# Reading the up products' tokens in turn, one store for a chunk, later reloads and a new order

## The chip, the cores and the metric

The kernel runs on one core of one Trainium2 chip. The metric is device time in microseconds (us), the median of several executions. An execution taken by the hardware profiler gives the trace from which the rows below are read.

## The reference

Two stages follow one another. The first is a gated recurrence for 4 batches, 8 heads, 768 tokens and 48 dimensions a head; the second is a feed-forward layer over the 3072 tokens, 384 wide inside and out, 2048 wide in the middle.

```python
for t in range(S):                                    # q, k, v, alpha: (4, 8, 768, 48)
    state = alpha[:, :, t, :, None] * state + np.einsum('bhd,bhe->bhde', k[:, :, t], v[:, :, t])
    y[:, :, t] = np.einsum('bhd,bhde->bhe', q[:, :, t], state)
x = y.transpose(0, 2, 1, 3).reshape(B * S, H * D)     # (3072, 384)
h = x @ w_in                                          # (3072, 2048)
sp = np.where(h > 20.0, h, np.log1p(np.exp(np.minimum(h, 20.0))))
out = (h * np.tanh(sp)) @ w_out                       # (3072, 384)
```

The weights come as 64-bit floats; everything else is 32-bit.

## The kernel before

**Chunks.** The recurrence is cut into 24 chunks. A chunk is 64 tokens of two batches at once: 128 rows, the first batch's 64 tokens and behind them the second's. For each chunk VectorE runs two scans over alpha and scales q and k, TensorE forms the scores, the products with v, the part from the state and the change of the state (lines 610, 633, 674, 755), and the 384 results of every token are written to the tile `xs` as an upper part and a remainder (lines 688 to 708). Six small transfers then put part of the rows in place (`move`, line 714).

**Units.** The feed-forward layer is cut into 106 units. A unit is one slice of 128 of the 2048 middle columns for two or four chunks, so 256 or 512 tokens. `up` (line 821) makes nine matmuls into one PSUM bank, three slices of the 384 inputs by three combinations of upper part and remainder, each with 256 or 512 columns of `xs` as the moving operand. ScalarE and VectorE then work on the result one after another: `exp` (line 830), `square` (833), `log` (836), `inverse` (839), `gate` on VectorE (842), `upper` (848), `lower` on VectorE (851). `down` (line 879) makes three matmuls of 384 columns for each chunk of the unit, with 128 tokens of `g` as weights; it gathers over the 16 slices in a PSUM bank of the chunk. After the last slice `result` (line 913) copies the bank to the tile `osb` (or adds to a part kept in SBUF first) and `store` (line 919) sends it to HBM in two transfers of 64 rows, one for each batch, because the two batches' tokens lie far apart in the output. Both go out on SyncE's queue (SP); for the last chunk, number 23, the second goes out on ScalarE's queue (`LAST_BY_ACT`).

**Weights.** Each of the 16 slices is loaded once (line 422), its 64-bit words are turned into an upper part and a remainder by VectorE and ScalarE (lines 437 to 480), and later it is loaded a second time (`wc`, line 495) for two sums by which ScalarE proves that the values fit the fast path (lines 504 and 507). The first loads and the reloads share two buffers, `stage`.

**Fillers.** Until a given time, TensorE is handed small matmuls without a use (line 937) where it would have nothing to do.

**The order.** Nothing is decided on the chip. A planner in the kernel's source walks through all tasks with a price for each (`COST`: time on the engine, time until others may use the result), a model of SP's queue (`SLACK` is added to each transfer's due time), and a key for each task: the number of the unit before which it is due plus a shift (`SHIFT`) found beforehand. On each engine the task that can begin first is next, and of several the one with the lowest key. `CHECK_FROM` and `CHECK_STEP` give the keys of the reloads, `EARLY_BANKS` says which PSUM banks a chunk uses. The order that comes out is what every engine then runs, strictly in that order: an instruction that waits for a transfer holds up everything behind it on its engine.

At the end the results of all checks are joined into one number, which decides whether a general path must run; it is not taken here.

Of the kernel before, what the change touches and what calls it, by code (L numbers as in the profile page):

```python
# [27 lines left out]
B, H, S, D = 4, 8, 768, 48  # L28
# [3 lines left out]
HALF = C // 2  # L32
# [31 lines left out]
CHECK_FROM = 45.0  # L64
# [6 lines left out]
    0: "o2 att att h h".split(),  # L71
    1: "att h o3 h att".split(),
    2: "o3 att o3 o0 o1".split(),
    3: "att att o3 o2 att".split(),
    4: "o0 att h".split(),
    7: "att o1 att".split(),
    8: "o3 att att".split(),
    9: "o1 att att".split(),
    10: "att o0 att".split(),
    11: "o2 att o1".split(),  # L80
    12: "o3 o0 att".split(),
    13: "h o1 att".split(),
    14: "o1 o0 o2".split(),
    15: "h att att".split(),
    16: "att h att".split(),
    17: "o0 h att".split(),
    18: "o0 att o2".split(),
    19: "o2 o0 att".split(),
    20: "att o2 att".split(),
    21: "att o1 o0".split(),  # L90
    22: "att o3 att".split(),
# [7 lines left out]
    },  # L99
    "unit": {  # L100
# [16 lines left out]
    },  # L117
    "weight": {
        0: -1.5121, 1: -4.3451, 2: -0.52089, 4: 0.30693, 5: 1.0304, 6: 3.2906, 7: 0.74523,
        8: 2.2474, 9: 2.1922, 10: 2.7782, 11: -2.8998, 12: 0.71473, 13: -2.0961, 14: 0.29398,  # L120
        15: -0.066785,
    },
    "weight check": {
        0: -0.41042, 1: -0.099631, 2: -3.9864, 3: 1.3786, 4: 0.10748, 5: 2.7189, 6: -0.74965,
        7: 3.7486, 8: 0.17213, 9: 2.0992, 12: 3.4975, 14: -1.471, 15: -6.7254,
    },
}
X_PE = 4
LAST_BY_ACT = (23,)
TURN_AT = 0.15  # L130
W_PE = 3
W_DVE = 3
# [160 lines left out]
SLACK, SLACK_FROM = (1.1, 0.4), 12.0  # L293
# [14 lines left out]
for _n in range(1, 5):  # L308
    _c = 128 * _n
# [896 lines left out]
```

## Time and profile before

| what | value |
|---|---|
| median of 3 runs | 509.14 us (508.57 to 509.17) |
| the profiled execution | 506.55 us |
| its span, first to last instruction | 504.8 us |
| mean granted clock of TensorE | 0.996 of full speed |
| TensorE busy | 487.5 us, 97% of the span |
| ScalarE busy | 393.2 us, 78% |
| VectorE busy | 323.9 us, 64% |
| moved by DMA | 56.83 MB |

The span leaves out what lies ahead of the first and behind the last instruction; the profiled execution took 1.75 us more than its span. The median of the timed runs lies 2.59 us above the profiled execution. A busy TensorE in this table includes the fillers, and the weight loads (431.5 us) overlap the matmuls.

### The profile page before, as it was taken

Reading aid. Unit: us, or ns where it says so; the run is one execution under the profiler, and the core shown is the slowest. Engines: PE = TensorE matmul, PEld = TensorE weight load, DVE = VectorE, ACT = ScalarE, POOL = GpSimd, SP = SyncE. Lnnn points to the kernel's source line nnn. Section 1 sums busy time; section 2 is a strip of 40 time slices with the busy share of each in tenths; the row PEclk is TensorE's granted clock in tenths of the full one; section 3 lists DMA queues with packets and bytes.
Section 4 is the critical chain, followed back from the end, with each engine's and each line's share of the span. In section 5 each row is a group of like instructions: output and inputs, shape, how many; then the busy total and the mean of one; then the engine's idle time right before and its main releaser. Section 6 shows DMA issues by size and latency. Waiting matters only on the chain.

```text
span 504.8 us, 12766 instructions
## 1 busy us (share of the span) xinstructions
PE 487.5 (97%) x5225; PEld 431.5 (85%) x5225; DVE 323.9 (64%) x632; ACT 393.2 (78%) x902; POOL 2.4 (0%) x12
## 2 busy tenths in 40 slices
PE   7979999999999998999999999999999999999993
PEld 4668999899998887889898889989888899889993
DVE  8989999999975777878534859323383333333231
ACT  2667988989989996979996677787666876886682
POOL 1000000000000000000000000000000000000000
PEclk9999999999999999999999999999999999999998
DMA  8765535433332755667410551000320000200002
GB/s 302 264 220 196 200 118 188 139 126 125 127 125 80 240 183 206 200 238 246 167 64 1 156 185 72 0 1 1 80 88 19 8 1 0 51 13 1 1 1 66
DMA packets 20463, 56.83 MB, mean 113 GB/s; under 512 B 4400, under 2 KB 12848, under 8 KB 20400
## 3 DMA queue, kind: packets, MB, share of 16 engines
q1 hardware_dynamic: 20320, 55.87, 33.0%
q8 instruction: 42, 0.69, 0.5%
q14 instruction: 21, 0.17, 0.1%
q10 hardware_dynamic: 80, 0.10, 0.1%
HBM read 48.87 MB, written 4.72 MB: 106 GB/s over the span
## 4 chain that ended last, share of the span: by engine, by line
PE 83%; DVE 5%; DMA 5%; ACT 2%; SPq 2%; issue 2%; DVEq 0%
PE bank L879 37%; PE bank L821 35%; PE bank L610 4%; DMA qka<-in_qka_dram 3%; PE bank L633 2%; PE bank L674 2%; SPq L714 2%; PE bank L755 2%; DMA wc<-in_wp_dram 1%; PE bank L476 1%; DVE qka L577 1%; DVE xs L693 1%; DVE state L794 1%; DVE probs L644 1%; DVE qka L587 0%
## 5 line engine op out<-in xcount | busy, mean ns | idle before, releaser
L879 PE MATMUL bank<-wo,g 128*128 128x384 f32 x1152 | 220.1, 339 | 0.5 <-DVE state L794 0.4
L821 PE MATMUL bank<-xs,wi 128*128 128x512 f32 (+1 forms) x954 | 215.9, 373 | 0.0
L879 PEld LDWEIGHTS bank<-wo,g 128*128 128x128 f32 x1152 | 201.0, 188 | 7.2 <-issue 1.1
L821 PEld LDWEIGHTS bank<-xs,wi 128*128 128x128 f32 x954 | 166.5, 188 | 28.1 <-DVE t L842 0.6
L842 DVE SCALAR_TENSOR_TENSOR t<-t,bank 128x512 f32<-128x512 f32 (+1 forms) x106 | 67.1, 634 | 96.8 <-ACT t L839 96.6
L851 DVE SCALAR_TENSOR_TENSOR g<-t,g 128x512 fp32r<-128x512 f32 (+1 forms) x106 | 66.2, 638 | 42.5 <-ACT g L848 42.4
L830 ACT ACTIVATE t<-bank 128x512 f32<-128x512 f32 (+1 forms) x106 | 58.8, 554 | 42.7 <-PE bank L821 41.5
L848 ACT ACTIVATE g<-t 128x512 fp32r<-128x512 f32 (+1 forms) x106 | 60.5, 586 | 24.5 <-PE bank L879 17.0
L836 ACT ACTIVATE t<-t,fifth 128x512 f32<-128x512 f32 (+1 forms) x106 | 72.2, 682 | 1.7
L833 ACT ACTIVATE t<-t 128x512 f32<-128x512 f32 (+1 forms) x106 | 62.5, 590 | 1.7
L839 ACT ACTIVATE t<-t 128x512 f32<-128x512 f32 (+1 forms) x106 | 62.3, 588 | 1.5
L564 DVE TENSOR_TENSOR_SCAN rest<-qka,behind 112x520 f32<-112x520 f32 x24 | 29.7, 1239 | 5.0 <-DMA qka<-in_qka_dram 4.9
L577 DVE TENSOR_TENSOR_SCAN qka<-qka,ahead 112x520 f32<-112x520 f32 x24 | 29.6, 1235 | 0.0
L688 ACT ACTIVATE xs<-bank 112x256 fp32r<-112x256 f32 x48 | 16.0, 380 | 8.5 <-PE bank L674 4.9
L644 DVE COPY_PREDICATED probs<-causal,bank 128x256 f32<-128x256 uint32 x48 | 18.9, 442 | 4.8 <-PE bank L633 3.3
L610 PE MATMUL bank<-qka,state 48*48 48x64 f32 (+1 forms) x704 | 20.5, 221 | 0.9 <-DVE part L906 0.4
L610 PEld LDWEIGHTS bank<-probs,v 64*48 64x48 f32 (+1 forms) x768 | 13.6, 127 | 9.1 <-issue 5.1
L830 ACT ACTIVATION_READ_ACCUMULATOR t<-bank 128x1 f32 x106 | 20.8, 196 | 0.0
L794 DVE TENSOR_TENSOR state<-bank,state 112x192 f32<-112x192 f32 x40 | 13.4, 354 | 11.1 <-PE bank L674 5.7
L610 PEld LDWEIGHTS bank<-qka,state 48*48 48x48 f32 (+1 forms) x704 | 15.8, 127 | 4.6 <-issue 1.8
L610 PE MATMUL bank<-probs,v 64*48 64x64 f32 (+1 forms) x768 | 17.0, 222 | 2.1 <-issue 1.7
L442 DVE SCALAR_TENSOR_TENSOR w_lead<-ws,w_lead 128x384 int32<-128x384 int32 x32 | 17.6, 555 | 0.0
(76 smaller groups left out, 334.8 us busy)
## 6 DMA issues: line engine op xcount, KB each, us to landing
qka<-in_qka_dram SPq DMA_DIRECT2D x22, 772.5 KB, 5.5
ws<-in_wp_dram SPq DMA_DIRECT2D x16, 768.0 KB, 4.3
wc<-in_wp_dram SPq DMA_DIRECT2D x16, 768.0 KB, 4.6
v<-in_vp_dram SPq DMA_DIRECT2D x24, 192.0 KB, 3.0
out_dram<-osb SPq DMA_DIRECT2D x31, 96.0 KB, 2.2
xs<-xs SPq DMA_DIRECT2D x144, 16.0 KB, 3.1
out_dram<-part SPq DMA_DIRECT2D x16, 96.0 KB, 2.9
qka<-in_qka_dram SPq DMA_DIRECT2D x2, 260.5 KB
```

The costliest lines, as they stand in the source:

```text
L564: nc.vector.tensor_tensor_scan(t[:, :0:-1], alpha()[:, :0:-1], behind[:, ::-1], 0.0, ALU.mult, ALU.max)
L577: nc.vector.tensor_tensor_scan(a, a, ahead, 0.0, ALU.mult, ALU.max)
L610: return nc.tensor.matmul(summed(x)[HALF * side : HALF * side + wide, j], weights(wide), moving, start=start, stop=stop, skip_group_check= ...
L821: nc.tensor.matmul(p[:, :N], wi[:, z, s, fs], x[:, s, :, a], start=m == 0, stop=m == len(passes) - 1,)
L830: nc.scalar.activation(wide(t), wide(h), AF.Exp, accum_out=uchk[:, at : at + 1])
L833: nc.scalar.activation(wide(t), wide(t), AF.Square, bias=1.0)
L836: nc.scalar.activation(wide(t), wide(t), AF.Ln, bias=fifth, scale=0.2)
L839: nc.scalar.activation(wide(t), wide(t), AF.Exp, scale=-1.0)
L842: nc.vector.scalar_tensor_tensor(wide(t), wide(t), 2.5, wide(h), ALU.subtract, ALU.mult)
L848: nc.scalar.activation(g.tile[:, 0, :N], wide(t), AF.Copy, scale=-0.4)
L851: late[mybir.EngineType.DVE] = nc.vector.scalar_tensor_tensor(g.tile[:, 1, :N], wide(t), -0.4, g.tile[:, 0, :N].bitcast(F32), ALU.mult, AL ...
L879: made = nc.tensor.matmul(o.tile[:, :DM], g.tile[:, a, j * C : (j + 1) * C], wo[:, z, f], start=begins and m == 0, stop=end and m == 2,)
```

## The change

Four edits are made together.

1. The moving operand of every `up` matmul is read through `by_token`: instead of 64 tokens of one batch and then 64 of the other, token 0 of the first batch, token 0 of the second, token 1 of the first, and so on. Neighbouring columns now lie 64 elements of 4 bytes apart in SBUF, in pairs, where they were next to each other. What follows (`h`, `t`, `g`, `osb`) has its tokens in that order.
2. With that a chunk's 128 result rows are stored by one transfer of 128 rows. The second store and the store on ScalarE's queue are gone: 24 transfers of 192 KB in place of 48 of 96 KB.
3. The reloads of the weights get keys from 62 on, where they had 45.
4. The order is made anew: prices, slack, banks and all shifts are replaced.

```diff
-CHECK_FROM = 45.0
+CHECK_FROM = 62.0
...
 EARLY_BANKS = {
-    0: "o2 att att h h".split(),
-    1: "att h o3 h att".split(),
...
+    0: "att o0 o1 att h".split(),
+    1: "att att h o2 h".split(),
...
 SHIFT = {
     "chunk": {
-        0: -2.6472, 1: 0.96249, 2: 0.82151, 3: -0.41315, 4: -2.1355, 5: -1.1454, 6: 0.33103,
...
+        0: -67.788, 1: -41.062, 2: -2.7315, 3: -0.50767, 4: 0.32113, 5: -0.14063, 6: 0.72447,
...
     "unit": {
...
-        100: 3.4911, 101: 0.030385, 102: 2.9112, 103: 2.5482, 104: 2.3446, 105: 2.2941,
+        96: 10.008, 97: 36.643, 98: 42.482, 99: 70.241, 100: 75.406, 101: 36.452, 102: 94.613,
+        103: 180.26, 104: 213.45, 105: 237.59,
     "weight": {
-        0: -1.5121, 1: -4.3451, 2: -0.52089, 4: 0.30693, 5: 1.0304, 6: 3.2906, 7: 0.74523,
+        0: -6.4516, 1: -18.694, 2: -0.0718, 3: -5.3782, 4: 0.59055, 5: -3.1028, 6: 0.22915,
...
     "weight check": {
-        0: -0.41042, 1: -0.099631, 2: -3.9864, 3: 1.3786, 4: 0.10748, 5: 2.7189, 6: -0.74965,
+        0: 3.4663, 1: 0.17532, 3: 5.129, 4: 4.2064, 5: 0.81532, 6: 4.6598, 7: 4.2295, 8: -5.8016,
...
-LAST_BY_ACT = (23,)
...
-SLACK, SLACK_FROM = (1.1, 0.4), 12.0
+SLACK, SLACK_FROM = (0.5, 0.3), 12.0
...
-    "load part": (0.47, 0.9), "load qk": (0.47, 1.75), "load q": (0.47, 2.45),
+    "load part": (0.47, 0.9), "load qk": (0.47, 1.75), "load q": (0.47, 3.2),
...
-    COST["up", _n] = (9 * (0.4333e-3 * _c + 0.009), 9 * (0.4333e-3 * _c + 0.009) + 0.205)
+    COST["up", _n] = (9 * (0.428e-3 * _c + 0.01), 9 * (0.428e-3 * _c + 0.01) + 0.205)
...
+    by_token = lambda t: t.rearrange("p n (x t) -> p n t x", x=2)
...
                 nc.tensor.matmul(
-                    p[:, :N], wi[:, z, s, fs], x[:, s, :, a], start=m == 0,
+                    p[:, :N], wi[:, z, s, fs], by_token(x[:, s, :, a]), start=m == 0,
                     stop=m == len(passes) - 1,
                 )
...
-            def store(n=n, osb=osb, x=0, by=nc.sync):
+            def store(n=n, osb=osb):
                 b, c = chunks[n]
-                by.dma_start(
-                    out[ds((2 * b + x) * S + c * HALF, HALF), :],
-                    osb.tile[HALF * x : HALF * x + HALF],
-                )
+                to = out[2 * b * S : 2 * (b + 1) * S, :].rearrange("(x s) d -> s x d", x=2)
+                nc.sync.dma_start(to[c * HALF : (c + 1) * HALF], osb.tile)
...
             add("SP", *COST["store"], k, store, [written], [osb])
-            if n in LAST_BY_ACT:
-                store1 = lambda store=store: store(x=1, by=nc.scalar)
-                add("ACT", *COST["store act"], k + 0.01, store1, [written], [osb])
-            else:
-                add("SP", *COST["store"], k + 0.01, lambda store=store: store(x=1), [written], [osb])
```

## Rows read from the trace of the kernel before

**Rows 1.** The page: engines' busy time, then TensorE's granted clock in 40 slices.

```profile
PE 487.5 (97%) x5225; PEld 431.5 (85%) x5225; DVE 323.9 (64%) x632; ACT 393.2 (78%) x902; POOL 2.4 (0%) x12
...
PEclk9999999999999999999999999999999999999998
```

**Rows 2.** Stretches: length, busy PE, PEld, DVE, ACT, POOL; clock, DMA share, GB/s.

```profile
10.00:20.00 10.00, 9.53 (x192) 6.00 (x189) 9.85 (x20) 5.87 (x19) 0.00 (x0) 1.00 0.68 272
20.00:30.00 10.00, 8.26 (x162) 5.84 (x161) 8.01 (x15) 4.64 (x13) 0.00 (x0) 1.00 0.86 286
30.00:40.00 10.00, 9.13 (x214) 7.65 (x213) 9.82 (x25) 7.74 (x25) 0.00 (x0) 1.00 0.60 201
40.00:50.00 10.00, 9.73 (x177) 8.09 (x176) 9.60 (x22) 7.86 (x23) 0.00 (x0) 1.00 0.57 201
...
190.00:200.00 10.00, 8.90 (x87) 7.64 (x86) 7.01 (x11) 5.58 (x12) 0.00 (x0) 1.00 0.68 259
200.00:225.00 25.00, 23.90 (x472) 21.13 (x473) 19.08 (x40) 21.66 (x54) 0.00 (x0) 1.00 0.57 184
...
300.00:350.00 50.00, 49.61 (x255) 45.07 (x254) 27.17 (x45) 37.48 (x76) 0.00 (x0) 1.00 0.08 28
```

**Rows 3.** The fillers (line 937) alone, by stretch: TensorE's two columns.

```profile
10.00:15.00 5.00, 2.47 (x14) 0.91 (x11) 1.00 1.00 417
15.00:20.00 5.00, 0.66 (x4) 0.31 (x4) 1.00 0.36 128
20.00:25.00 5.00, 1.81 (x9) 0.60 (x7) 1.00 0.93 318
...
40.00:50.00 10.00, 1.95 (x11) 1.07 (x11) 1.00 0.57 201
```

**Rows 4.** The chain that ended last, in order of time: start, us, what.

```profile
19.50 0.67 PE bank L937 x4
...
24.15 0.65 PE bank L476 x2
...
145.45 4.10 PE bank L821 x18
149.55 4.19 PE bank L879 x24
...
190.12 7.49 DMA wc<-in_wp_dram
```

**Rows 5.** TensorE's groups, shapes kept apart: busy us, mean ns.

```profile
L821 PE MATMUL bank<-xs,wi 128*128 128x512 f32 x774 | 190.7, 393 | 0.0
L821 PE MATMUL bank<-xs,wi 128*128 128x256 f32 x180 | 25.2, 286 | 0.0
```

**Rows 6.** Line 504 (reloads' first sum): ns min/median/max, first and last start.

```profile
L504 ACT ACTIVATE wc<-wc x16: 888/906/947, 149.1 to 259.4; 128x768 f32<-128x768 f32 x16
L504 ACT ACTIVATION_READ_ACCUMULATOR wc<-wc x16: 185/190/251, 149.9 to 260.2; 128x1 f32 x16
```

**Rows 7.** Timeline of 197 to 202 us: start, length, instruction, idle before it.

```profile
197.63 0.90 ACT L504 ACTIVATE wc<-wc 128x768 f32<-128x768 f32 x1 [2.63 <-DMA wc<-in_wp_dram]
...
200.35 0.69 DVE L842 SCALAR_TENSOR_TENSOR t<-t,bank 128x512 f32<-128x512 f32 x1 [2.05 <-ACT t L839]
...
201.10 0.60 PE L755 MATMUL bank<-ident,qka 112*128 112x112 f32 x4 [1.83 <-DVE t L842]
```

**Rows 8.** Timeline of the end, same columns.

```profile
496.03 4.34 SPq L919 DMA_DIRECT2D out_dram<-osb  x7
...
497.38 0.19 ACT L913 ACTIVATION_READ_ACCUMULATOR osb<-bank 128x1 f32 x1
...
497.60 0.55 ACTq L919 DMA_DIRECT2D out_dram<-osb  x1
```

**Rows 9.** DMA issues of the page: count, KB each, us to landing.

```profile
v<-in_vp_dram SPq DMA_DIRECT2D x24, 192.0 KB, 3.0
out_dram<-osb SPq DMA_DIRECT2D x31, 96.0 KB, 2.2
```

More of the change, by code (lines that the diff above doesn't have):

```diff
@@ L70 @@
 EARLY_BANKS = {
-    0: "o2 att att h h".split(),
-    1: "att h o3 h att".split(),
[L73 to L83, printed above, removed]
+    0: "att o0 o1 att h".split(),
+    1: "att att h o2 h".split(),
+    2: "o2 o1 att o0 att".split(),
+    3: "att o0 o3 att att".split(),
+    4: "att att o2".split(),
+    5: "att o2 att".split(),
+    10: "o1 o2 o3".split(),
+    11: "att o1 att".split(),
+    12: "o1 o2 o0".split(),
+    13: "att o3 att".split(),
+    14: "att o2 o0".split(),
     15: "h att att".split(),
[L85 to L88, printed above, removed]
+    16: "o0 o1 att".split(),
+    17: "o1 att o3".split(),
+    18: "o0 o1 att".split(),
+    19: "att att h".split(),
     20: "att o2 att".split(),
-    21: "att o1 o0".split(),
-    22: "att o3 att".split(),
+    21: "att o0 h".split(),
+    23: "att h att".split(),
 }
@@ L94 @@
     "chunk": {
[4 rows of a table removed]
[4 rows of a table added]
     },
     "unit": {
[16 rows of a table removed]
[16 rows of a table added]
     },
     "weight": {
-        0: -1.5121, 1: -4.3451, 2: -0.52089, 4: 0.30693, 5: 1.0304, 6: 3.2906, 7: 0.74523,
-        8: 2.2474, 9: 2.1922, 10: 2.7782, 11: -2.8998, 12: 0.71473, 13: -2.0961, 14: 0.29398,
-        15: -0.066785,
+        0: -6.4516, 1: -18.694, 2: -0.0718, 3: -5.3782, 4: 0.59055, 5: -3.1028, 6: 0.22915,
+        7: 3.6276, 8: -0.93908, 9: 4.1863, 10: -1.3406, 11: -0.89088, 12: 0.60959, 13: 2.7395,
+        14: 2.9243, 15: 3.4437,
     },
     "weight check": {
-        0: -0.41042, 1: -0.099631, 2: -3.9864, 3: 1.3786, 4: 0.10748, 5: 2.7189, 6: -0.74965,
-        7: 3.7486, 8: 0.17213, 9: 2.0992, 12: 3.4975, 14: -1.471, 15: -6.7254,
+        0: 3.4663, 1: 0.17532, 3: 5.129, 4: 4.2064, 5: 0.81532, 6: 4.6598, 7: 4.2295, 8: -5.8016,
+        9: 1.9332, 10: -0.19251, 11: -6.9069, 12: -0.12023, 13: -4.9148, 14: 4.4556, 15: 14.881,
     },
@@ L292 @@
 DMA_FIRST, DMA_LAST = 1.67, 0.3
-SLACK, SLACK_FROM = (1.1, 0.4), 12.0
+SLACK, SLACK_FROM = (0.5, 0.3), 12.0
 COST = {
-    "load part": (0.47, 0.9), "load qk": (0.47, 1.75), "load q": (0.47, 2.45),
-    "load v": (0.47, 0.6), "load w": (0.45, 2.2), "move": (0.625, 0.15), "store": (0.62, 0.7), "store act": (0.62, 2.7),
-    "cold fill": (0.321, 0.36), "fill": (0.1635, 0.2), "off": (0.21, 0.37), "w off": (0.93, 1.05), "lead": (0.27, 0.37), "bits": (0.47, 0.585), "w hi": (0.415, 0.53), "w lo": (0.95, 1.08),
+    "load part": (0.47, 0.9), "load qk": (0.47, 1.75), "load q": (0.47, 3.2),
+    "load v": (0.47, 0.6), "load w": (0.45, 2.35), "move": (0.625, 0.15), "store": (0.62, 0.9),
+    "cold fill": (0.321, 0.36), "fill": (0.1635, 0.2), "off": (0.21, 0.37), "w off": (0.965, 1.09), "lead": (0.27, 0.37), "bits": (0.47, 0.585), "w hi": (0.415, 0.53), "w lo": (0.95, 1.08),
     "w check": (0.89, 1.1),
@@ L301 @@
     "state": (0.272, 0.4), "state0": (0.21, 0.35), "decay": (0.469, 0.605), "mask": (0.335, 0.49),
-    "scores0": (0.72, 0.85), "scores": (0.95, 1.09), "y0": (1.175, 1.29), "y": (1.407, 1.53),
+    "scores0": (0.7, 0.83), "scores": (0.92, 1.06), "y0": (1.15, 1.27), "y": (1.37, 1.5),
     "y last": (0.935, 1.05), "turn": (0.35, 0.68),
@@ L305 @@
     "x hi": (0.265, 0.415), "x lo": (0.333, 0.45),
-    "down": (0.521, 0.79), "stash": (0.36, 0.5), "join": (0.468, 0.59), "result": (0.485, 0.61),
+    "down": (0.5235, 0.79), "stash": (0.36, 0.5), "join": (0.468, 0.59), "result": (0.485, 0.61),
 }
```

35 rows, old and new, of the table SHIFT are left out of this document.

## Prediction

> **What bounds the kernel now.** [...] Over the whole span TensorE sets the time; the question is in which stretches it loses any. The table by stretches answers that. Of the gaps between the first 10 us and the end, nearly all lie in two places: TensorE stands idle for 0.47 + 1.74 + 0.87 + 0.27 = 3.35 us between 10 and 50 us and for 1.10 + 1.10 = 2.20 us between 190 and 225 us; the next in size, 300 to 350 us, has 0.39 [rows 2]. Busy is not useful, though: 14 + 4 + 9 + 11 = 38 fillers run in the stretches shown between 10 and 50 us [rows 3], at 0.67 / 4 = 0.168 us each [rows 4], so 6.4 us more are lost there. VectorE is 80 to 98% busy in those 40 us, so this early part waits for what VectorE must do first. The third loss is the end: the last chunk's result is copied by 497.57 us, while seven stores in a row on SP go on to 500.37; then the last of them lands and the program closes [rows 8, 9]. So there are three places to win: about 9.7 us early, 2.2 us in the middle, and the end. Everything else is work of TensorE that the order cannot shorten.
>
> **The up products' reads.** No instruction is added. The 774 matmuls of 512 columns and 180 of 256 [rows 5] read the same elements in another sequence: neighbouring columns are 64 elements of 4 bytes apart, where they were adjacent. Now 18 of the long ones take 4.10 us, 0.228 us each or 0.445 ns a column [rows 4]; all 954 come to 774 x 0.228 + 180 x 0.114 = 197 us. No row shows a matmul that reads with such a step. [...] For the upper bound I take the slowest stream of the trace that resembles it, the plain 32-bit matmuls of line 476: 0.65 us for two of 384 columns, 0.85 ns a column [rows 4], 1.9 times as much, so up to 0.9 x 197 = 177 us more. The ends lie far apart; the row nearest in line, data and column count is that of the product itself, so I take nothing. If that cover is gone nothing hides the price: TensorE is full there [rows 2], and every 5.2 ns a matmul costs 5 us.
>
> [...]
>
> **The stores.** Now SP's seven stores at the end take 4.34 us; one issue takes 0.55 (the one on ScalarE's queue), so they follow each other every (4.34 - 0.55) / 6 = 0.63 us and the last begins at 496.03 + 4.34 - 0.55 = 499.82 [rows 8]. With 2.2 us to land [rows 9] that is 502.0. After the change SP has four stores for the last four chunks. The fourth cannot begin before 496.03 + 3 x 0.63 = 497.92, nor before chunk 23's copy is done at 497.38 + 0.19 = 497.57 [rows 8]; so 497.92. How long 192 KB take to land is bounded by the store of 96 KB, 2.2 us, and by the load of 192 KB, 3.0 us [rows 9]; I take the middle, 2.6, and get 500.5. The end comes 1.5 us earlier, between 1.1 and 1.9. The copies and the last matmul of the check are over before that, so nothing else is late next. Earlier in the run 20 stores fewer go through SP, 12.6 us of its time; no store is waited for by TensorE there, so I give that nothing, except that SP's queue is freer for the moves and loads between 170 and 225 us.
>
> **The reloads.** Each is one transfer of SP and two passes on ScalarE, 0.906 + 0.190 us each [rows 6], 2.2 us in all and 35 us for 16. They now run between 149 and 260 us [rows 6]. In the middle gap the trace shows what one of them does: issued at 190.12, it is 7.49 us on the chain [rows 4]; ScalarE stands 2.63 us before it, VectorE's gate then waits 2.05 us for ScalarE, and TensorE stands 1.83 us behind the gate [rows 7]. ScalarE runs in order, so the late transfer blocks the next units' activations. With keys 17 units later, the reloads yield to the units and chunks of this stretch. They move to where 28 GB/s flow instead of 259 and 184 and ScalarE is 75% busy (300 to 350 us against 190 to 225) [rows 2]: 44 units from number 62 on, at (4.10 + 4.19) / 2 = 4.15 us of TensorE each [rows 4], are 182 us with a quarter free, 45 us for 35 of work. So they fit, with little to spare. What is won lies between nothing (another wait takes this one's place) and the 2.20 us of both stretches; some of it may come back in a stretch that ScalarE now fills, so I take 1.5. Loads of the first kind lose nothing, as they have their buffers before.
>
> **The new order.** The early 9.7 us are what a better sequence of chunks, weights and units could win at the most; a worse one could lose as much, since VectorE is nearly full there. The row nearest to a new order is the old order's own, so I stay close to zero. What tips me to a gain is that the new prices lie on the trace (a group of three `down` matmuls costs 4.19 / 8 = 0.524 us [rows 4], the diff goes from 0.521 to 0.5235), and an order made with truer prices is likelier to have fewer gaps. I take a tenth of it, 1.0 us, with 4 us to either side for the range. The shorter slack is the risk: a transfer that is booked 0.6 us sooner leaves the engine waiting more often.
>
> **The sum.** 1.5 + 1.5 + 1.0 = 4.0 us. The span goes from 504.8 to 500.8, the profiled execution from 506.55 to 502.55. The timed runs' median lies 2.59 us above the profiled execution, and I keep that distance: 509.14 - 4.0 = 505.1 us.
>
> **The rivals.** (a) The reads cost. Place: every `up` matmul. [...] For it speaks that no row shows such a step; against it, that the new plan prices nine long products at 9 x (0.428e-3 x 512 + 0.01) = 2.06 us, the 2.05 that the chain shows for adjacent columns, so it was laid out for no penalty; that is an assumption of the plan, not a row. It decides from 4.2 ns a matmul, 2% of it: there the 4.0 us are eaten. Chance 0.08. (b) The order wins nothing, and a wait of the same size takes the place of the one at 197 us: only the stores are left, 507.6. For it speaks that VectorE stays as full as it was. Chance 0.13. (c) The new order strays from the chip: with the shorter slack, reloads are waited for in the full stretch after 225 us. Each such wait gives TensorE a loss like that of 190 to 225 us, 2.2 us; three of them without the early gain give 509.14 - 3.0 + 6.6 = 512.7, two of them 510.5. It decides from two. For it speaks that 35 of 45 us are taken there; against it, that the transfers have the queue nearly to themselves. Chance 0.12. (d) The early part finds much more, 2 to 4 us beyond my tenth: 501 to 503. Chance 0.12. (e) The single transfer lands as late as two did, because its rows are fetched no faster: 506.6, inside my forecast's own band.
>
> **How the numbers follow.** My forecast, 503 to 507, has 0.55. A measurement of this kernel tells changes of about 0.2%, 1.0 us, from none, so faster means below 508.1 and slower above 510.2. Faster: 0.55, 0.12 of (d) and 0.08 of (b), 0.75. Within 0.2%: 0.05 of (b) and 0.04 of (c), 0.09. Slower: 0.08 of (a) and 0.08 of (c), 0.16. The range runs from 501.5 to 509.5; it leaves out (a), most of (c) and the lowest part of (d), somewhat under 0.2.
>
> **What would show it.** Reads: the group of 512 columns keeps 2.05 us for nine in the chain; more than 2.1 is rival (a). Stores: four on SP at the end, none on ScalarE's queue, the last begun 1.9 us after the first. Reloads: line 504 starts later than 149 us and ends after 350, and 190 to 225 us show TensorE full; a new idle stretch of 1 us or more with a reload ahead of it is rival (c). Order: idle and fillers between 10 and 50 us fall together below 9.7 us. The prediction is wrong if the reads have a price, or if the order brings back more than the 3.0 us of the stores and the reloads.

## Result and the profile after

| | before | changed |
|---|---|---|
| median of the timed runs, side by side | 508.86 us (507.41 to 509.17) | 500.11 us (499.68 to 500.50) |
| ratio, with its 95% interval | 1 | 0.9847 (0.9807 to 0.9887) |
| the profiled execution | 506.55 us | 500.14 us |
| its span | 504.8 us | 498.3 us |

The changed kernel is 1.5% faster. The direction was forecast; the size was not: 4.0 us were predicted and about 8 were won, and 500.1 lies below the range of 501.5 to 509.5. In a second set of runs the two medians were 507.77 and 500.44, ratio 0.9847 (0.9778 to 0.9916). The old kernel's own runs spread widely, from 502.4 to 512.0 us in the largest set, so a gain below is given as a ratio with its interval or between two kernels that ran side by side; where it is taken between two sets of runs, the text says so. In the largest set the five longest runs of the old kernel, 510.0 to 512.0 us, show a mean granted clock of TensorE of 0.986 to 0.990 and are left out of the ratios; the five shortest show 0.995 to 0.996.

The page and the DMA issues of the changed kernel, in the order of [rows 1] and [rows 9]; the third line is the page's chain by engine:

```profile
PE 481.0 (97%) x5229; PEld 431.9 (87%) x5229; DVE 326.0 (65%) x632; ACT 396.8 (80%) x902; POOL 2.4 (0%) x12
...
PEclk9999999999999999999999999999999999999998
...
PE 55%; DVE 20%; ACT 19%; issue 4%; DMA 1%; ACTq 0%; DVEq 0%
...
out_dram<-osb SPq DMA_DIRECT2D x16, 192.0 KB, 2.3
```

TensorE is busy for 6.5 us less with four fillers more, while VectorE and ScalarE are busy for 2.1 and 3.6 us more with as many instructions as before. So something made TensorE's instructions shorter and the other two engines' longer. The groups of the `up` products, as in [rows 5], show the first:

```profile
L819 PE MATMUL bank<-xs,wi 128*128 128x512 f32 x774 | 181.7, 383 | 2.8 <-DVE t L840 2.4
L819 PE MATMUL bank<-xs,wi 128*128 128x256 f32 x180 | 24.3, 281 | 0.1
```

and the chain that ended last, as in [rows 4], has the price of one:

```profile
326.80 3.88 PE bank L819 x18
330.68 4.24 PE bank L877 x24
334.92 1.94 PE bank L819 x9
```

Eighteen long products take 3.88 us where they took 4.10: 0.2156 us each in place of 0.228. The read in turn, which the prediction priced at nothing, is quicker than the read of neighbours.

The stretches, with the columns of [rows 2]:

```profile
10.00:20.00 10.00, 8.98 (x190) 5.82 (x188) 9.89 (x21) 6.15 (x19) 0.00 (x0) 1.00 0.78 284
20.00:30.00 10.00, 9.93 (x178) 7.46 (x177) 9.27 (x20) 5.23 (x15) 0.00 (x0) 1.00 0.74 271
30.00:40.00 10.00, 9.33 (x166) 6.72 (x163) 9.29 (x21) 7.57 (x25) 0.00 (x0) 1.00 0.54 182
40.00:50.00 10.00, 9.63 (x222) 8.78 (x223) 9.84 (x25) 7.61 (x24) 0.00 (x0) 1.00 0.75 272
190.00:200.00 10.00, 10.00 (x55) 9.48 (x55) 7.37 (x12) 6.51 (x14) 0.00 (x0) 1.00 0.61 242
200.00:225.00 25.00, 23.98 (x594) 20.84 (x593) 20.22 (x44) 22.10 (x55) 0.00 (x0) 1.00 0.69 245
...
250.00:300.00 50.00, 48.93 (x603) 43.73 (x602) 24.86 (x47) 42.19 (x93) 0.00 (x0) 1.00 0.26 88
```

Between 10 and 50 us TensorE stands idle for 1.02 + 0.07 + 0.67 + 0.37 = 2.13 us, 1.2 less than before, but 45 fillers (19, 16 and 10 in the first three stretches) run there where there were 40 (38 in the stretches that [rows 3] shows). At 0.168 us each, idle time and fillers come to 9.7 us in place of 10.1: next to nothing was found in the early part. The gap at 197 us is gone, about 1 us is left behind 200, and 1.07 us of new idle time stand between 250 and 300 us (0.63 us at 272.7 behind `gate`, 0.34 at 278.9 behind `result`, all of it after the last reload's sums).

The reloads did not move. Line 502 is their first sum, with the columns of [rows 6]:

```profile
L502 ACT ACTIVATE wc<-wc x16: 898/1002/1297, 145.5 to 260.8; 128x768 f32<-128x768 f32 x16
```

They start between 145.5 and 260.8 us, before from 149.1 to 259.4, and the median has grown from 906 to 1002 ns.

The end, with the columns of [rows 8]:

```profile
489.53 0.49 ACT L911 ACTIVATE osb<-bank 128x384 f32<-128x384 f32 x1 [1.99 <-PE bank L877]
...
490.14 2.48 SPq L918 DMA_DIRECT2D out_dram<-osb  x4
...
491.49 0.19 ACT L911 ACTIVATION_READ_ACCUMULATOR osb<-bank 128x1 f32 x1
```

Four stores go out on SP, as forecast. Yet from the first of these copies to the end of the span it is 498.3 - 489.53 = 8.77 us; before it was 9.37. What holds the end is told by the instructions of the closing branch, line 1129 (ns min/median/max, first and last start):

```profile
L1129 SPq EVENT_SEMAPHORE  x8: 17/17/17, 494.5 to 495.1; - x8
...
L1129 DVEq COMPARE_BRANCH  x1: 84/84/84, 493.3 to 493.3; - x1
...
L1129 DVEq EVENT_SEMAPHORE  x1: 21/21/21, 497.3 to 497.3; - x1
```

SP is through its last waits by 495.1 us. VectorE's queue reaches the branch at 493.3 and comes out of it at 497.3, 4.0 us later; in the old kernel it took 0.6 us (499.04 to 499.66).

### The profile page after: what moved, and what is told of

Read it like the earlier page. It is cut to its first block, busy times and chain, and to the rows that moved or that the text cites. A ratio compares the mean times of both kernels' runs of the same rounds, so it can differ in the third digit from the quotient of the medians.

```text
span 498.3 us, 12735 instructions
## 1 busy us (share of the span) xinstructions
PE 481.0 (97%) x5229; PEld 431.9 (87%) x5229; DVE 326.0 (65%) x632; ACT 396.8 (80%) x902; POOL 2.4 (0%) x12
## 4 chain that ended last, share of the span: by engine, by line
PE 55%; DVE 20%; ACT 19%; issue 4%; DMA 1%; ACTq 0%; DVEq 0%
PE bank L877 24%; PE bank L819 21%; PE bank L608 4%; ACT t L834 3%; DVE t L840 3%; ACT t L828 3%; DVE g L849 2%; DVE w_lead L445 2%; DVE w_lead L440 2%; ACT t L831 2%; ACT wc L502 2%; ACT g L846 2%; ACT wc L505 2%; ACT t L837 2%; DVE rest L562 2%
## 5 line engine op out<-in xcount | busy, mean ns | idle before, releaser
L877 PE MATMUL bank<-wo,g 128*128 128x384 f32 x1152 | 218.4, 339 | 1.1 <-DVE xs L691 1.1
L819 PE MATMUL bank<-xs,wi 128*128 128x512 f32 (+1 forms) x954 | 206.1, 364 | 2.8 <-DVE t L840 2.4
L849 DVE SCALAR_TENSOR_TENSOR g<-t,g 128x512 fp32r<-128x512 f32 (+1 forms) x106 | 67.2, 643 | 40.6 <-ACT g L846 40.4
L562 DVE TENSOR_TENSOR_SCAN rest<-qka,behind 112x520 f32<-112x520 f32 x24 | 29.8, 1242 | 0.4 <-DMA qka<-in_qka_dram 0.3
L445 DVE SCALAR_TENSOR_TENSOR w_lead<-ws,w_lead 128x384 int32<-128x384 int32 x32 | 19.3, 605 | 0.0
L440 DVE SCALAR_TENSOR_TENSOR w_lead<-ws,w_lead 128x384 int32<-128x384 int32 x32 | 19.0, 608 | 0.0
L608 PEld LDWEIGHTS bank<-probs,v 64*48 64x48 f32 (+1 forms) x768 | 13.4, 127 | 6.3 <-issue 2.1
```

What stands on the lines that cost most here:

```text
L562: nc.vector.tensor_tensor_scan(t[:, :0:-1], alpha()[:, :0:-1], behind[:, ::-1], 0.0, ALU.mult, ALU.max)
L608: return nc.tensor.matmul(summed(x)[HALF * side : HALF * side + wide, j], weights(wide), moving, start=start, stop=stop, skip_group_check= ...
L819: nc.tensor.matmul(p[:, :N], wi[:, z, s, fs], by_token(x[:, s, :, a]), start=m == 0, stop=m == len(passes) - 1,)
L849: late[mybir.EngineType.DVE] = nc.vector.scalar_tensor_tensor(g.tile[:, 1, :N], wide(t), -0.4, g.tile[:, 0, :N].bitcast(F32), ALU.mult, AL ...
L877: made = nc.tensor.matmul(o.tile[:, :DM], g.tile[:, a, j * C : (j + 1) * C], wo[:, z, f], start=begins and m == 0, stop=end and m == 2,)
```

## Experiments

**The read alone, in the old order.** Edit of the old kernel:

```diff
+    by_token = lambda t: t.rearrange("p n (x t) -> p n t x", x=2)
...
-                    p[:, :N], wi[:, z, s, fs], x[:, s, :, a], start=m == 0,
+                    p[:, :N], wi[:, z, s, fs], by_token(x[:, s, :, a]), start=m == 0,
```

> The kernel before with the reading in turn alone; order, two stores and reloads as before, so that the rows of the output stand in another sequence. Theory R (the reading itself makes each up product shorter, whatever the order): nine matmuls of 512 columns take 1.94 us on the chain where they took 2.05, 774 x 12 ns + 180 x 5 ns = 10 us less work on TensorE, and the run is 6 to 10 us faster than before, 499 to 503. Rival O (the new order made the room, and the shorter products come from it, for instance from fewer engines reading SBUF beside them): nine still take 2.05 us and the time is that of before within 1 us.

Nine long products took 1.94 us, as in the changed kernel, but the time did not follow: 506.12 us, ratio 0.9999 (0.9963 to 1.0035). A quicker `up` is worth nothing measurable while the rest is as it was; the interval leaves room for 1.8 us. The reload at 197 us shows why in part; it is as late as before [rows 7], and the 1.80 us behind it are still there (timeline, columns of [rows 7]):

```profile
198.57 0.91 ACT L505 ACTIVATE wc<-wc 128x768 f32<-128x768 f32 x1 [2.29 <-DMA wc<-in_wp_dram]
...
201.29 0.69 DVE L843 SCALAR_TENSOR_TENSOR t<-t,bank 128x512 f32<-128x512 f32 x1 [2.02 <-ACT t L840]
...
202.04 0.60 PE L756 MATMUL bank<-ident,qka 112*128 112x112 f32 x4 [1.80 <-DVE t L843]
```

Right behind that gap TensorE's granted clock falls in this trace (columns of [rows 2]):

```profile
200.00:203.00 3.00, 1.20 (x50) 0.93 (x43) 1.71 (x4) 3.00 (x9) 0.00 (x0) 1.00 0.00 0
203.00:207.00 4.00, 4.00 (x120) 3.91 (x111) 1.99 (x6) 2.97 (x9) 0.00 (x0) 0.57 0.44 105
```

The old kernel's trace shows two values, 1.00 and, in its last 4 us (500.8 to 504.8), 0.50; by these a mean of 0.57 is, as an estimate, 3.4 of the 4 us at 0.50. The same is seen from 29 to 33 us (0.57), behind 4 us in which TensorE was busy for 1.76. The old kernel's trace has gaps at both places (busy for 2.26 us from 25 to 29 us, 1.83 us idle before 201.10) and no such fall: 1.00 from 29 to 33 and from 203 to 207 us. How much of the gain is lost by this is not shown.

**The changed kernel with the old read.** Edit of the changed kernel, the same line turned back: `by_token(x[:, s, :, a])` becomes `x[:, s, :, a]`.

> The changed kernel with adjacent columns read as before; the new order and the single stores stay, so the rows of the output stand in another sequence. Theory R: nine long matmuls take 2.05 us again and the time goes back by 8 to 11 us, to 508 to 511; the order and the stores by themselves are worth 2 us or less. Rival O: the time stays at that of the changed kernel, 500 to 502.

503.21 us (501.98 to 503.94), ratio to the old kernel 0.9922 (0.9887 to 0.9958). The changed kernel lies at 500.1 and 500.4 in its two sets, which are other sets than this one, so under the new order the read is worth some 3 us. Counted in the two traces, the 1401st of the 2106 `up` and `down` matmuls begins at 344.9 us with the old read and at 345.3 with the new one; from there to the end of the last it is 148.8 and 145.4 us. The whole gain of 3.4 us arises in the last third, where TensorE alone sets the pace.

**The single store alone, planned anew.** Edit of the old kernel: edit 2 of the change, and no other; the planner then finds another order, which differs from about 185 us on.

> The kernel before with one store of 128 rows for a chunk alone; read and order as before, so that the rows land in other places of the output. The prediction's price for the end is 1.5 us: 507.3. The two profiles show less: from the first copy of the last results to the end it is 9.37 us before and 8.77 after, so theory E (the end after the last store grew, and only 0.6 us are left) gives 508.2. The last store should begin 1.9 us after the first in either case; what differs is what lies behind it.

510.45 us, ratio 1.0052 (1.0010 to 1.0094): slower. The end itself is 510.7 - 503.86 = 6.84 us from the same copy, 2.5 less than before, so the stores do give back time; the order that the planner made out of the old shifts loses more, with 1.68 + 1.93 us of idle TensorE between 250 and 350 us.

**Read and single store, planned anew.** Edits 1 and 2 in the old kernel.

> The kernel before with the reading in turn and the single stores, the order, the reloads' keys and all prices as before. Theory N (the new order is what turns the shorter products into time, and what keeps TensorE's gaps short enough for its clock): 504 to 507, with a wide spread and stretches of TensorE's lower clock in the profile. Rival S (read and stores explain the gain together, and each alone had been spoilt by the other's absence): 500 to 501.

508.07 us, ratio 1.0016 (0.9981 to 1.0052). This mixes two edits with a third, the order, that nobody chose. The next two take the order out.

**The same two, the order kept.** The planner is left to think that there are two stores, and the second one issues nothing:

```diff
-                by.dma_start(
-                    out[ds((2 * b + x) * S + c * HALF, HALF), :],
-                    osb.tile[HALF * x : HALF * x + HALF],
-                )
+                if x == 0:
+                    to = out[2 * b * S : 2 * (b + 1) * S, :].rearrange("(x s) d -> s x d", x=2)
+                    nc.sync.dma_start(to[c * HALF : (c + 1) * HALF], osb.tile)
```

With the old read first; its output rows then stand in another sequence.

> The kernel before with the single store, and every other instruction in the order of before on every engine (the planner still plans two stores, the second issues nothing); the rows land in other places of the output. In the first run with the single store the planner had put out another order from about 200 us on. Theory A (the single store by itself shortens the end, as that run's profile showed, 6.84 us from the first copy to the end where before takes 9.37): 2 to 2.5 us less than before, a ratio of 0.995 to 0.996. Rival B (the larger store delays the moves behind it in the queue, and the end's gain is lost): the same as before or slower.

502.28 us (501.26 to 503.00), beside 507.04 of the old kernel in that set; ratio 0.9885 (0.9808 to 0.9962). The store alone is worth 4.8 us by the medians, between 1.9 and 9.7 by the interval. In the profiled executions the last `down` product begins 1.0 us earlier than in the old kernel, and from the first of the last four copies to the end it is 6.9 us in place of 9.4. The gap behind 197 us is gone with the store alone (columns of [rows 2]):

```profile
190.00:200.00 10.00, 10.00 (x61) 9.03 (x63) 8.00 (x13) 8.13 (x19) 0.00 (x0) 1.00 0.67 257
```

Set side by side product by product, this trace is 2.2 us behind the old one before that gap and 0.4 us ahead behind it: 2.6 us are won there. It was behind through two losses that are not explained by the edit: a granted clock of 0.57 in the mean from 29 to 33 us and 1.22 us of TensorE's idle time at 179 us. Then with the new read:

> The read in turn and the single store together, with the order of before kept on every engine. Theory A2 (the old order can use both, and the earlier run was spoilt by its new plan): the end's 2.5 us and some 2 to 3 us of the read, a ratio of 0.989 to 0.993, still 3 us and more above the changed kernel. Rival N (without the new order nothing but the end is won): a ratio of 0.995 to 0.998.

498.91 us (496.76 to 499.07), ratio 0.9827 (0.9751 to 0.9902): another 3.4 us, and 1.2 to 1.5 us below the medians of the changed kernel in its other two sets. SyncE's queue in this kernel (timeline; start, length, what):

```profile
172.04 1.32 SPq L922 DMA_DIRECT2D out_dram<-part  x2
...
174.10 2.10 SPq L922 DMA_DIRECT2D out_dram<-part  x2
...
177.47 8.97 SPq L715 DMA_DIRECT2D xs<-xs  x12
...
187.57 0.90 SPq L496 DMA_DIRECT2D wc<-in_wp_dram  x2
...
217.09 5.09 SPq L715 DMA_DIRECT2D xs<-xs  x6
```

and the same stretch of the old kernel:

```profile
171.99 3.24 SPq L919 DMA_DIRECT2D out_dram<-part  x4
...
175.95 1.10 SPq L919 DMA_DIRECT2D out_dram<-part  x2
...
178.23 1.11 SPq L919 DMA_DIRECT2D out_dram<-part  x2
179.44 9.54 SPq L714 DMA_DIRECT2D xs<-xs  x12
...
221.48 5.90 SPq L714 DMA_DIRECT2D xs<-xs  x6
```

Eight stores stand ahead of the twelve moves where four are enough. With four, the reload that was issued at 190.12 us [rows 4] goes out at 187.57, and the last six moves shown 4.4 us earlier, at 217.09. ScalarE's wait for reloads is gone: the group of line 505 has 0.0 us of idle time before it, where the same group (line 504) had 3.9 us in the old kernel and 2.3 us with the read alone; with the store alone it has 0.0 too (groups of the old kernel and of this one: busy us, mean ns, idle before).

```profile
L504 ACT ACTIVATE wc<-wc 128x768 f32<-128x768 f32 x16 | 14.6, 910 | 3.9 <-DMA wc<-in_wp_dram 3.9
```

```profile
L505 ACT ACTIVATE wc<-wc 128x768 f32<-128x768 f32 x16 | 16.7, 1046 | 0.0
```

And the stretches, with the columns of [rows 2]:

```profile
190.00:200.00 10.00, 9.99 (x146) 8.97 (x147) 8.09 (x13) 8.28 (x20) 0.00 (x0) 1.00 0.45 184
200.00:225.00 25.00, 25.00 (x448) 22.79 (x438) 20.08 (x41) 22.37 (x55) 0.00 (x0) 1.00 0.70 242
```

These stretches, 2.20 us idle before [rows 2], are all but full. In the old kernel TensorE waited not for a store but, by way of ScalarE and `gate`, for a reload that stood behind stores on the same queue.

**How a moving operand may be read.** Edit of the changed kernel: each weight slice gets another sequence of the columns, so the sums of a token come out mixed.

```diff
+                r = x[:, s, :, a]
+                step = lambda k: r.rearrange("p n (x t) -> p n t x", x=k)
...
+                elif f % 8 == 3:
+                    nc.tensor.matmul(p[:, :N], w, step(4), **go)
```

> The changed kernel with another sequence of columns for each weight slice: up reads adjacent columns, columns 64, 8, 4, 2, 32 or 16 elements apart, or two runs of 64 in three dimensions; down reads adjacent columns or columns 192, 4 or 2 elements apart. The sums of a token come out mixed, so the output is not the reference's. [...] Rival D (the number of dimensions of the access decides): the runs of 64 are as fast as the steps. Rival F (only far steps help): 1.94 at 64 and 32 elements, 2.05 at 16, 8 and 4.

One execution, 691.72 us. The chain of one stretch holds all forms (start, us, what):

```profile
389.37 3.88 PE bank L831 x9
393.25 4.15 PE bank L833 x9
...
408.39 4.24 PE bank L835 x9
412.63 2.10 PE bank L896 x12
414.73 3.96 PE bank L837 x9
418.68 1.95 PE bank L898 x12
420.64 2.06 PE bank L823 x9
...
423.07 2.10 PE bank L827 x9
...
429.33 2.45 PE bank L829 x9
```

Nine `up` products of 512 columns, by the distance of neighbouring columns:

| line | read | nine take |
|---|---|---|
| 823 | adjacent, 4 bytes | 2.06 us |
| 825 | two streams, 256 bytes apart (the change) | 1.94 us (at 305.31 us; the chain of the changed kernel above has the same) |
| 827 | the two batches one after the other | 2.10 us |
| 829 | four streams, 128 bytes apart | 2.45 us |
| 837, 831, 833, 835 | 8, 16, 32, 64 streams: 64, 32, 16, 8 bytes | 3.96, 3.88, 4.15, 4.24 us |

The `down` products behave alike: twelve take 2.10 us adjacent (line 896), 1.95 in two streams 768 bytes apart (line 898), and 4.17 and 4.09 at steps of 16 and 8 bytes (lines 900 and 902). Neither rival of the expectation held: the two batches one after the other (2.10 us) are not as fast as two streams (1.94), and at 128 bytes nine take 2.45 us and not 1.94. Two streams are quicker than one (1.94 and 2.06 us), four are slower (2.45), and eight and more take about twice as long (3.88 to 4.24). With more streams the step gets shorter in these forms, so number and distance are not told apart, except that two streams save the same 12.5 ns a matmul at 256 and at 768 bytes. Rival (a) of the prediction, that the changed read costs, is out: it is the fastest of all (1.94 us).

**`down` in turn as well.** If two streams save 12.5 ns a matmul in `up`, they should in `down`. Edit of the changed kernel, with the columns of the second weights laid out beforehand so that the result stays the same:

```diff
+    in_turn = lambda t: t.rearrange("p (x d) -> p d x", x=2)
...
-                        o.tile[:, :DM], g.tile[:, a, j * C : (j + 1) * C], wo[:, z, f],
+                        o.tile[:, :DM], g.tile[:, a, j * C : (j + 1) * C], in_turn(wo[:, z, f]),
...
-    wp[:, :, 1] = w_out.reshape(NFF, P, DM)
+    wp[:, :, 1] = w_out.reshape(NFF, P, DM // 2, 2).transpose(0, 1, 3, 2).reshape(NFF, P, DM)
```

> The changed kernel, and the down products too read their moving operand in turn: the columns of the second weight matrix are laid out so that columns 192 apart are neighbours, and the result comes out in the old sequence. The patterns run showed 1.95 us for twelve such matmuls where adjacent columns take 2.10. Theory R: twelve take 1.95 us; 1152 x 12.5 ns = 14 us less work of TensorE. If TensorE set the pace everywhere, 486; by what the read was worth under the new order (3 of 10 us) a third of it, 495 to 497. Rival W (in a steady stretch ScalarE, at three quarters, is next and nothing more is won): 499.5 or more.

Twelve take 1.95 us, 13.4 us less busy time (218.4 to 205.0), and 498.51 us (498.39 to 498.86) come out of it, ratio 0.9807 (0.9738 to 0.9875); the changed kernel in the same set gave 500.44. So 1.9 of 13 us reach the end. Most of the rest stands as idle time: TensorE is busy for 43.38 of the 47 us from 130 to 177, where the changed kernel has 45.94. And two groups of other engines have grown. First the kernel with the new order and the old read, then this one (groups: busy us, mean ns of one, idle before):

```profile
L440 DVE SCALAR_TENSOR_TENSOR w_lead<-ws,w_lead 128x384 int32<-128x384 int32 x32 | 17.2, 549 | 0.0
...
L502 ACT ACTIVATE wc<-wc 128x768 f32<-128x768 f32 x16 | 14.6, 912 | 1.7 <-DMA wc<-in_wp_dram 1.7
```

```profile
L441 DVE SCALAR_TENSOR_TENSOR w_lead<-ws,w_lead 128x384 int32<-128x384 int32 x32 | 20.3, 647 | 0.0
...
L503 ACT ACTIVATE wc<-wc 128x768 f32<-128x768 f32 x16 | 18.8, 1174 | 1.9 <-DMA wc<-in_wp_dram 1.9
```

Both passes read every second 32-bit word. They take 549 and 912 ns while TensorE reads neighbours, 608 and 1052 with `up` in turn, 647 and 1174 with `down` in turn too. The sizes vary from trace to trace (a second one of the changed kernel has 593 and 1066), the direction does not; by what way the reads slow the passes is not shown. The scans, which read neighbours, stay as they were (1239 ns in the old kernel, 1242 in the changed one).

**In turn only late, only early.** If the slower passes are paid for in the first part and the gain is made in the last, the read in turn should be kept to units from 33 on:

```diff
-                    p[:, :N], wi[:, z, s, fs], by_token(x[:, s, :, a]), start=m == 0,
+                    p[:, :N], wi[:, z, s, fs], by_token(x[:, s, :, a]) if at >= 33 else x[:, s, :, a], start=m == 0,
```

> The changed kernel with the reading in turn from unit 33 on alone (73 of 106 units, from about 135 us on); units before that read adjacent columns, so tokens of the two kinds of units are mixed in the sums and the output is not the reference's. VectorE is full up to 140 us, and with the reading in turn its two passes over the weights' 64-bit words (a step of two elements) take 0.606 us where they took 0.549, 4.5 us in all with the third pass. Theory V (reading in turn takes SBUF time from other engines' stepped reads, and so gives back in VectorE's stage what it saves): these passes are at 0.55 us again, and the time is 1 to 4 us below the changed kernel, 496.5 to 499.5, although 33 units save less on TensorE. Rival S (the saving on TensorE counts there too): 33 units' saving, about 3 us of TensorE time, is missing and the time is 501 to 503.

> The complement: the reading in turn up to unit 32 alone; the sums are mixed as in the run before. Theory V: VectorE's passes stay at 0.60 us, nothing is won later, 503 to 507, at or above the run with the old read (503.2). Rival S: about 3 us of saving, 500 to 502.

Late: 499.62 us (499.24 to 499.75), ratio 0.9859 (0.9816 to 0.9902). VectorE's passes are back at 556 and 557 ns, the reloads' sums, which run later, still take 1063 and 1107. Early: 504.83 us, ratio 0.9970 (0.9936 to 1.0003), with the passes at 591 and the sums back at 911 and 897. The place of the loss is shown by that, and so is the place of the gain: early reads in turn win nothing (503.21 us without any, in another set). But late alone is only 0.5 to 0.8 us better than everywhere, by medians of different sets, and just above the 499.5 that was expected at most; the slower passes cost little here.

**The closing branch.** The old and the changed program differ by 11 in the number of instructions in VectorE's queue. Edit of the changed kernel, twelve writes without a use behind VectorE's last work:

```diff
+    pad = const.tile([P, 1], F32, name="pad")
+    with tc.issue_after(late[mybir.EngineType.DVE].ins):
+        for _ in range(12):
+            nc.vector.memset(pad, 0.0)
```

> The changed kernel with twelve small fills on VectorE behind its last product, so that its closing branch stands at the 720th instruction of its queue where it stood at the 708th (the kernel before: 719th). In the changed kernel VectorE passes that branch 4.0 us after reaching it, in the kernel before 0.7 us, and the program ends right after. Theory P (where the branch stands among VectorE's instructions decides whether what follows is at hand): VectorE is through in under 1 us and the run ends 2 to 3 us earlier, 497 to 498. Rival T (it goes by what else happens at that time): 4 us again, 500.

497.97 us (496.95 to 498.17), ratio 0.9795 (0.9727 to 0.9863), 2.5 us faster than the changed kernel with twelve instructions more. The branch:

```profile
L1133 DVEq COMPARE_BRANCH  x1: 84/84/84, 492.1 to 492.1; - x1
...
L1133 DVEq EVENT_SEMAPHORE  x1: 21/21/21, 492.7 to 492.7; - x1
```

0.6 us in place of 4.0. So what stands ahead of the branch decides how long it takes, as theory P has it; the reason that the theory gives is shown by no run. From the branch to the next instruction of VectorE's queue it is 4.0 us in the changed kernel, 3.9 in its second trace, 4.2 with the old read and 4.1 with `down` in turn; it is 0.6 us in the old kernel, with the single store alone planned anew, with both edits in the old order, and here. The queue has 708 instructions in the changed kernel, 719 in the old one and 720 here.

**The changed kernel again**, beside these:

> The changed kernel once more, beside the others of this set. 499.5 to 501 as at first. Against it the run with the old read (503.2) gives the worth of the read under the new order: theory R2 (the read saves 10 us of TensorE's work, but under either order most of it turns into waiting where VectorE or ScalarE sets the pace) says about 3 us; if this run comes out at 503, the read is worth nothing under either order.

500.44 us (500.28 to 501.31), ratio 0.9847 (0.9778 to 0.9916).

**Both additions**, `down` in turn and the twelve writes:

> The changed kernel with the down products in turn too (498.5 alone) and the twelve small fills at the end (498.0 alone). If the two add up, as one lies in the middle and one in the close: 500.4 - 1.9 - 2.5 = 496.0.

496.57 us (495.83 to 498.35), ratio 0.9812 (0.9765 to 0.9859); the lowest median of these kernels. The lowest ratio is that of the twelve writes alone, 0.9795, and the two intervals overlap, so what `down` in turn adds to them is not shown. Its chain is no longer TensorE's for the most part:

```profile
PE 46%; ACT 22%; DVE 22%; DMA 4%; issue 4%; SPq 1%; ACTq 0%; DVEq 0%
```

**New prices.** The same kernel, with the measured durations of `up`, `down`, the weights' passes and the sums in `COST`, and everything planned anew without a new search for shifts:

```diff
-    "down": (0.5235, 0.79), "stash": (0.36, 0.5), "join": (0.468, 0.59), "result": (0.485, 0.61),
+    "down": (0.4875, 0.754), "stash": (0.36, 0.5), "join": (0.468, 0.59), "result": (0.485, 0.61),
...
-    COST["up", _n] = (9 * (0.428e-3 * _c + 0.01), 9 * (0.428e-3 * _c + 0.01) + 0.205)
+    COST["up", _n] = (9 * (0.4167e-3 * _c + 0.0023), 9 * (0.4167e-3 * _c + 0.0023) + 0.205)
```

> The same with four prices of the planner brought to what the runs show (up 9 x 0.2156 us, down 3 x 0.1625, VectorE's stepped passes 0.53 + , the reloads' sums 1.1), so that another order comes out from the same shifts. Theory N says that the order is worth as much as the products: a plan with true prices should be at least as good, 493 to 496. Rival C (the shifts were found for the old prices, and a plan without a search for new ones is a random one): 497 to 503.

504.65 us, ratio 0.9966 (0.9939 to 0.9992): 8 us lost with truer prices. The shifts fit the prices that they were found with better than this second set; TensorE's mean granted clock was lower as well, 0.992 in the profiled execution and 0.986 to 0.995 in the ten runs, where the kernel with both additions has 0.999 and 0.993 to 0.999.

## Why the prediction was wrong

Two terms that the prediction put at nothing, the reads and the stores in the middle of the run, gave some 5.7 us between them; the two that it counted beside the stores of the end, the reloads' key and the order, gave none. The direction came out right, but 2.5 of the 4.0 us that carried it stood on these last two.

| step | forecast | measured |
|---|---|---|
| reads in turn | 0 | -3.4 us in the old order with single stores (502.28 to 498.91), -2.8 to -3.1 in the new; nothing with two stores (ratio 0.9999) |
| single store, at the end | -1.5 us | -0.6 us in the changed kernel, -2.5 where the branch is quick |
| single store, in the middle | nothing | some -2.3 us: the 4.8 of the store alone (1.9 to 9.7), less 2.5; 2.6 at the gap in its trace |
| reloads' key | -1.5 us | 0, it leaves the order as it is |
| new order | -1.0 us, 4 either way | +1.2 to +1.5 us by medians of different sets, the branch in it; the ratios' intervals overlap |
| profiled execution to median | 2.59 us, kept | 0.0 us |

**Reads.** This is the step whose reasoning failed. The prediction weighed nothing against up to 177 us more, and a gain was in none of its cases; the read in turn took 12.5 ns off a long product (0.228 to 0.2156 us), and off a `down` product of 384 columns as well (2.10 / 12 = 0.175 us adjacent, 1.95 / 12 = 0.1625 in two streams). So the old read was the slower one, which no row of the old trace could tell. The size needs the place: 10.1 us of busy time are saved (190.7 + 25.4 with the old read in the new order, 181.7 + 24.3 with the new), and 3 arrive: between 10 and 400 us TensorE's idle time grows from 3.3 to 7.6 us, and TensorE's part of the chain that ended last is 55% where the old kernel's page has 83%: up to 345 us a quicker TensorE soon waits for VectorE and ScalarE, whose stepped passes have become slower besides.

**Stores.** The term is mis-sized. The end was read rightly: 2.3 us for 192 KB to land where 2.6 were taken, and where VectorE's branch is quick it is 6.9 us in place of 9.4 from the first of the last copies to the end, 2.5 less, somewhat more than the 1.9 of the upper bound. In the changed kernel the end gives only 0.6 us, because the branch is late next; the prediction looked at the copies and the check's last matmul for that and not at the branch. What failed is the sentence "no store is waited for by TensorE there, so I give that nothing": on a queue that runs in order it is not the store that is waited for but the moves and loads behind it. The stores of the first parts sit in front of the very reload that [rows 7] had shown (it goes out at 190.12 us behind eight of them and at 187.57 behind four), and with four stores fewer there the stall is gone whose cure the prediction gave to the reloads' key.

**Reloads.** "With keys 17 units later, the reloads yield" was argued and is wrong. From either kernel's source the planner makes the same order, task for task on every engine, with 45 and with 62, under the old shifts and under the new ones: a key decides between tasks that could begin together and in what sequence buffers are handed out, and here this one changes neither. The gap at 197 us went, by way of the stores and not of the key: in the kernel with the old key, the old order and single stores it is gone too. The last reload's first sum begins at 260.8 us, where an end after 350 was forecast. Rival (c), more reload waits behind 225 us, did not come: ScalarE waits for no reload there, and the idle time between 250 and 300 us comes after them. Nor did (e): the single transfer lands about as fast as half of it did (2.3 and 2.2 us).

**Order.** A tenth of the early loss was forecast as a gain. Early, 0.4 us were found, so rival (d), whose time of 501 to 503 us lies nearest to the result, is not how it came about. In all, the new order lies 1.2 to 1.5 us above the old one with both edits, by medians of different sets; the ratios, 0.9847 and 0.9827, have intervals that overlap, so a loss is not shown. The branch alone is about 2.5 of it; without it (497.97, in another set) it stands within the runs of the old order with both edits (496.76 to 499.07). "An order made with truer prices is likelier to have fewer gaps" is not borne out by the one test, which kept the shifts and lost 8 us.

**The base.** The forecast starts from a median of three, 509.14, and keeps its distance of 2.59 us to the profiled execution. The old kernel's median came out between 506.2 and 508.9 in later sets, and the changed kernel has no such distance (500.14 profiled, 500.11 the median). From the profiled execution, the 4.0 us would have given 502.55: 2.6 of the 5.0 us of error are this step, the rest is the sum's.

**What stays open.** The three effects, -4.8, -3.4 and +1.2 to +1.5, add up to 6.7 to 7.0 us; the side-by-side differences are 7.3 and 8.8. The parts also depend on their sequence: the read gives nothing with two stores and 3.4 us with one, so taken read first all of the gain falls to the store. The old kernel's spread is as large as what is missing. Part of it has a mark in the record: in three of the four sets of the experiments its longer runs are those with the lower granted clock (0.986 to 0.989 in the longest of a set, 0.994 to 0.997 in the shortest), in the fourth they are not. That the gaps at 25 and 197 us let the clock fall in some executions, and that single stores help by closing the second, fits the trace of the read alone (0.57 behind either gap) and is not shown. Nor was it settled why one stream of columns is slower than two.

## What to carry to other kernels

Count an instruction's cost on an in-order queue by what stands behind it, not by who waits for it: half as many stores were worth about as much in the middle of the run, by way of a reload, as at the end, and a look at the stores themselves could not show it. The way a matmul's moving operand is read may be a lever: two alternating streams are worth a trial (0.2156 us in place of 0.228 for 512 columns here), more than two were slower; the gain reached the end only where TensorE alone sets the pace. Change one part with the order held fixed before judging it, for an edit that makes a planner plan anew is measured together with an order that nobody chose.

## What the chip showed unexpectedly

- The moving operand in two streams, 256 or 768 bytes apart, runs 12.5 ns a matmul faster than in adjacent columns (0.2156 and 0.228 us for 512 columns, 0.1625 and 0.175 for 384); in four streams it takes 0.27 us, in eight to 64 streams 0.43 to 0.47 us.
- While TensorE reads in two streams, passes of VectorE and ScalarE over every second 32-bit word take longer: 549 to 608 and 647 ns, 912 to 1052 and 1174 ns in three traces, 11 to 29%; over all traces with `up` in turn throughout, VectorE's take 577 to 657 ns. Scans over neighbours do not (1239 ns in the old kernel, 1242 in the changed one).
- The same closing branch took VectorE's queue 4.0 us in the changed kernel, with 708 instructions in that queue, and 0.6 us in the old one with 719 and in the changed one with 720; the twelve more made the kernel 2.5 us faster.
- With the same order of instructions TensorE's granted clock fell behind a gap in one execution and not in another (203 to 207 us: a mean of 0.57 of full speed with the read alone, 1.00 in the old kernel).
